# Moving stores to another queue, k casts to another engine and weight loads to a later point in a linear-attention + MLP kernel

## The chip, the cores and the metric

The kernel runs on one core of one Trainium2 chip. The metric is the time of one execution in microseconds (us) on the device. A profiled execution also has a span, which is shorter than its time; positions such as "at 54.27" are microseconds from the start of the span.

The engines are TensorE (PE; its weight loads are PEld), VectorE (DVE), ScalarE (ACT), GpSimd (POOL) and SyncE (SP). Each works through its own list of instructions in order, as the stall described below shows. Tiles whose names begin with `ps_` lie in PSUM, the memory into which TensorE's results go here. A semaphore is a counter on which an instruction waits until another has raised it. A DMA is a transfer between memories; it is issued from one engine's list; a "q" behind an engine's name (ACTq, SPq) marks the engine's sequencer, which does the issuing.

A run counts as slow when it is over 1.5% above the fastest of its kernel; ratios and the medians below are of fast runs.

## The reference, cut to what matters

Causal linear attention with a decay, over 4 batches, 8 heads, 768 positions and a head size of 64, and then an MLP on its 3072 x 512 output.

```python
for b in range(nb):                       # blocks of 64 positions
    intra = einsum('bhic,bhjc->bhij', qb, kb) * Dmask     # decay lam^(i-j), causal
    intra = einsum('bhij,bhjd->bhid', intra, vb)
    inter = einsum('bhid,bhde->bhie', qb * lam_pow, kv_state)
    out[:, :, sl] = intra + inter
    kv_state = lam_block * kv_state + einsum('bhsd,bhse->bhde', kb * rev_pow, vb)
x = out.transpose(0, 2, 1, 3).reshape(3072, 512)
h = x @ w_in                              # 512 x 2048
g = h / (1 + exp(-1.702 * h))
return g @ w_out                          # 2048 x 512, float32
```

## The kernel before

The work is cut into six waves of 128 positions (512 tokens with the four batches). A wave's attention is done in four head pairs. A pair has four steps: casts, transposes (`step_a`), scores, mask and state (`step_b`), and the attention output (`step_c`). Wave 0's attention stands alone at the start, while weights load. The attention of each later wave is interleaved with the MLP of the wave ahead of it, so that TensorE has matmuls to do between the steps.

```python
def do_cast(w, p):
    kf, qf, vf = loaded.pop((w, p))
    ...
    for h in range(2):
        hd = 2 * p + h
        nc.vector.tensor_scalar(ks[:, :, h, :], kf[:, :, h, :], scalar1=k_pow[:, hd : hd + 1], scalar2=None, op0=MUL)
        if w <= 1:
            nc.scalar.activation(qs[:, :, h, :], qf[:, :, h, :], COPY, scale=q_pow[:, hd : hd + 1])
        else:
            nc.vector.tensor_scalar(qs[:, :, h, :], ...)
    nc.gpsimd.tensor_copy(v_sb[w % 2][p][:, :, 0:3:2, :], vf)

def step_a(w, p):                    # 8 transposes of ks and qs, then one copy out of PSUM
    ...
    nc.vector.tensor_copy(kq, ps_t)

def step_b(w, p):                    # 8 score matmuls, 2 masks, 4 state matmuls, 2 state updates
    ...
    nc.vector.scalar_tensor_tensor(sm, s2[h], inv_pow[...], mask.to_broadcast([P, B, P]), op0=MUL, op1=MUL)
    ...
    nc.vector.scalar_tensor_tensor(new[hs, :, hs], old[hs, :, hs], blk_pow[...], ps_kv[hs, :, hs], op0=MUL, op1=ADD)

def mlp2(w, g, j):
    ...
    if j == FFC // CW - 1:
        o = op.tile([P, d_model], f32, tag="o", name="o_sb")
        nc.vector.tensor_copy(o, ps_out)
        (nc.sync if w else nc.scalar).dma_start(out=out[r0 : r0 + P, :], in_=o)     # wave 0: on ScalarE

...
for p in range(NP):                  # wave 0
    do_cast(0, p)
    if p == 2:
        load_weights()               # 3 w_in and 4 w_out chunks, issued by GpSimd
        sync_behind_weights()        # SyncE waits for the third w_out chunk
        load(1)                      # wave 1's k, q, v, issued by SyncE
    step_a(0, p)
    if p:
        step_c(0, p - 1)
    step_b(0, p)
...                                  # then 8 memsets on GpSimd (v_sb and kv_sb of wave 1)
...                                  # wave w's main list: 19 mlp1 items, 16 mlp2 items; load(w + 2) at its start
```

## Time and profile before

The median of the runs is 260.73 us (260.08 to 260.99).

The page of the profile gives each engine's busy time, then the busy share in forty slices of 6.5 us, in tenths. PEclk is the clock that TensorE was granted, in tenths of full speed.

```profile
PE 219.7 (84%) x1478; PEld 115.6 (44%) x1504; DVE 104.8 (40%) x208; ACT 85.1 (33%) x153; POOL 27.2 (10%) x59
...
PE   0374899807665899999999999999999999999993
...
PEclk9999999975777999999999999999999999999999
```

TensorE is at nine tenths or more nearly throughout after the first 14 slices. What can be won lies in the first 14 slices, and there are two weak places: the beginning, and the stretch from about 50 to 90 us.

The same, cut by stage (the windows view): wave 0's attention; wave 0's MLP as far as it runs alone; wave 1's attention; and the first 35 us of the steady waves. The columns are the window, its length, the busy time of each engine with its instructions, the granted clock, the DMA share and GB/s.

```profile
core 0: us, PE busy (x) PEld busy (x) DVE busy (x) ACT busy (x) POOL busy (x), PEclk, DMA share, GB/s
0.00:26.90 26.90, 11.30 (x105) 8.55 (x107) 12.38 (x20) 12.77 (x27) 14.98 (x39) 1.00 0.98 191
26.90:51.00 24.10, 23.07 (x109) 10.61 (x111) 2.56 (x5) 10.49 (x19) 1.22 (x2) 1.00 0.99 190
51.00:88.10 37.10, 20.31 (x145) 10.97 (x146) 15.03 (x29) 5.18 (x11) 5.52 (x9) 0.72 0.90 210
88.10:123.60 35.50, 34.30 (x258) 18.68 (x263) 18.23 (x39) 12.26 (x21) 0.61 (x1) 1.00 0.10 34
```

The steady stretch has TensorE busy for 34.30 of 35.50 us. Wave 1's attention is the outlier: 37.10 us long, TensorE busy for 20.31, at a mean clock of 0.72.

What happens there (the timeline; columns: start, duration, engine, line, operation, out<-in, shape and count, and in brackets the idle time before it and what ended that):

```profile
46.05 0.69 DVE L236 COPY o_sb<-ps_out 128x512 f32<-128x512 f32 x1 [18.50 <-PE ps_out L232]
...
51.03 0.39 PE L167 MATMUL ps_t<-ident,ks 128*128 128x128 bf16 x4
...
54.27 4.48 ACTq L238 DMA_DIRECT2D out_dram<-o_sb  x2
...
58.79 0.91 ACT L156 ACTIVATE qs<-qf,q_pow 128x256 bf16<-128x256 f32 x2 [15.60 <-DMA qf<-in_q_dram]
...
59.76 0.61 PE L167 MATMUL ps_t<-ident,qs 128*128 128x128 bf16 x4 [8.34 <-ACT qs L156]
...
63.71 0.61 PE L180 MATMUL ps_s<-kq 64*128 64x128 bf16 x8
...
66.75 0.62 DVE L154 TENSOR_SCALAR ks<-kf,k_pow 128x256 bf16<-128x256 f32 x2
...
67.43 0.40 PE L167 MATMUL ps_t<-ident,ks 128*128 128x128 bf16 x4 [2.57 <-DVE ks L154]
...
70.62 0.61 PE L180 MATMUL ps_s<-kq 64*128 64x128 bf16 x8
```

There are two troubles.

**A store in front of a cast.** The first output tile of wave 0 is ready at 46.05 + 0.69 = 46.74. Its store issues only at 54.27. ScalarE's next instruction, the q cast of wave 1's first pair, runs at 58.79, after two stores, and TensorE stands for 8.34 us for want of it. Why a store waits is told by the order of instructions in the built program with the semaphores that each waits for (not a profile):

```
SyncE     44 L79 DMACopy qf<-in_q_dram 128x4x64 [waits DMAHW6_49]
SyncE     50 L79 DMACopy qf<-in_q_dram 128x4x64 [waits DMAHW4_49,Activation_49]
ScalarE   31 L238 DMACopy out_dram<-o_sb 128x512 [waits DMAHW6_49,DVE_49]
ScalarE   32 L238 DMACopy out_dram<-o_sb 128x512 [waits DMAHW4_49,DVE_49]
ScalarE   33 L156 Activation qs<-qf,q_pow 128x4x64
```

The program rotates eight semaphores among all DMAs issued by SyncE and ScalarE, and a DMA waits until the one that used its semaphore last has landed. So the first store waits for a load of wave 1's last pair, and the second for a load of wave 2, although it needs neither's data. The chain of waits (start, duration, what) names the second of these loads:

```profile
54.56 3.71 DMA qf<-in_q_dram
...
58.35 0.40 ACTq L238
...
58.79 0.92 ACT qs L156 x2
```

The Trainium skill, "DMA: Bandwidth & Descriptors", section "Anatomy of one DMA — SWDGE (gpsimd) path", says that the DMA engines themselves don't wait on semaphores: any such wait happens on the issuing sequencer before the DMA is dispatched. That is what makes the wait costly here. It stands in ScalarE's list, and the trace agrees: ScalarE's arithmetic is idle for 15.60 us ahead of the q cast at 58.79.

**A ring of one pair after another.** The scores of the first two pairs are at 63.71 and 70.62, 6.91 us apart. The next pair's k cast is in VectorE's list behind this pair's mask (1.40 us) and state update (0.98), so the next transposes come 3.7 us after the scores (67.43), and their copy and the next scores come behind those.

**The beginning.** The timeline of the last pair of wave 0, by engine:

```profile
20.71 2.91 DVE L154 TENSOR_SCALAR ks<-kf,k_pow 128x256 bf16<-128x256 f32 x2
...
20.23 0.36 POOL L298 MEMSET v_sb_145<- 128x256 bf16 x1
...
22.64 0.58 POOL L298 MEMSET kv_152<- 128x512 bf16 x1
...
26.87 1.48 PE L222 MATMUL ps_h<-xT,w_in_157 128*128 128x512 bf16 x5 [0.22 <-issue]
```

Two k casts take 2.91 us here and 0.62 at 66.75. During the long ones GpSimd runs eight memsets.

### The profile page before, as it was taken

To read this page: it belongs to the slowest core of one execution; us is meant where nothing else is said; L and a number is where in the kernel's file an instruction comes from. 1 tells how busy PE (TensorE), PEld (TensorE's weight loads), DVE (VectorE), ACT (ScalarE), POOL (GpSimd) and SP (SyncE) were. 2 spreads that over 40 slices of the span, in tenths; PEclk is the share of its full clock that TensorE was granted. 3 is DMA by queue.
4 is the path that set the end of the run, shared out by engine and by line. 5 is a ranking of instruction groups with operands and counts; after the bars stand their busy time and mean duration, and the time that the engine had idled before them with its cause. 6 is when DMAs were issued, how large, how long until landed. Compare 5 with 4: busy or idle time off the path is not lost.

```text
span 260.2 us, 3823 instructions
## 1 busy us (share of the span) xinstructions
PE 219.7 (84%) x1478; PEld 115.6 (44%) x1504; DVE 104.8 (40%) x208; ACT 85.1 (33%) x153; POOL 27.2 (10%) x59
## 2 busy tenths in 40 slices
PE   0374899807665899999999999999999999999993
PEld 0253444403333445555455554555554455544441
DVE  0457200202455947371854555564527425110121
ACT  6543564001320165311455012551106530146200
POOL 6185000011111000000011000010000000000000
PEclk9999999975777999999999999999999999999999
DMA  5999997999997200012795114990111001210022
GB/s 134 235 192 204 205 160 175 212 247 263 233 240 170 65 20 3 0 40 83 176 221 130 40 43 125 235 205 3 54 69 40 0 3 42 83 40 0 0 83 81
DMA packets 83350, 29.62 MB, mean 114 GB/s; under 512 B 76676, under 2 KB 79748, under 8 KB 83332
## 3 DMA queue, kind: packets, MB, share of 16 engines
q1 hardware_dynamic: 79060, 24.13, 37.6%
q0 software_dynamic: 3696, 4.19, 9.8%
q10 hardware_dynamic: 576, 1.05, 1.1%
q8 instruction: 12, 0.20, 0.3%
q14 instruction: 6, 0.05, 0.1%
HBM read 27.27 MB, written 6.29 MB: 129 GB/s over the span
## 4 chain that ended last, share of the span: by engine, by line
PE 69%; DMA 10%; SPq 9%; DVE 3%; issue 3%; ACT 2%; POOL 1%; ACTq 0%; DVEq 0%; POOLq 0%
PE ps_out L232 30%; PE ps_h L222 26%; SPq L79 9%; DMA w_out_162<-in_moe_w_out_dram 8%; PE ps_t L167 4%; PE ps_o L209 4%; PE ps_s L180 3%; PE ps_kv L189 2%; PE ps_o L207 2%; DMA qf<-in_q_dram 1%; DMA vf<-in_v_dram 1%; ACT g_sb L225 1%; DVE sm L183 1%; DVE ks L154 1%; DVE o_sb L236 1%
## 5 line engine op out<-in xcount | busy, mean ns | idle before, releaser
L225 ACT ACTIVATE g_sb<-ps_h 128x512 bf16<-128x512 f32 x96 | 56.0, 597 | 54.4 <-PE ps_h L222 53.6
L232 PEld LDWEIGHTS <-g_sb 128*128 128x128 bf16 x384 | 37.4, 101 | 40.5 <-issue 3.3
L183 DVE SCALAR_TENSOR_TENSOR sm<-ps_s,inv_pow,mask 128x512 bf16<-128x512 f32 x48 | 33.8, 747 | 34.6 <-PE ps_s L180 34.6
L236 DVE COPY o_sb<-ps_out 128x512 f32<-128x512 f32 x24 | 16.6, 691 | 73.2 <-PE ps_out L232 73.0
L222 PE MATMUL ps_h<-xT,w_in_159 128*128 128x512 bf16 x185 | 44.7, 379 | 0.4
L212 ACT CAST xT<-ps_o 128x512 bf16<-128x512 f32 x24 | 14.0, 585 | 76.0 <-PE ps_o L209 75.6
L169 DVE COPY kq<-ps_t 128x1024 bf16<-128x1024 bf16 x24 | 16.6, 692 | 38.5 <-PE ps_t L167 38.5
L167 PE MATMUL ps_t<-ident,ks 128*128 128x128 bf16 x96 | 10.2, 234 | 20.6 <-DVE ks L154 20.6
L222 PEld LDWEIGHTS <-w_in_159 128*128 128x128 bf16 x192 | 18.1, 98 | 19.1
L232 PE MATMUL ps_out<-w_out_162,g_sb 128*128 128x512 bf16 x95 | 26.0, 398 | 0.2 <-issue 0.2
L222 PE MATMUL ps_h<-xT,w_in_157 128*128 128x512 bf16 x94 | 23.1, 381 | 3.6 <-ACT g_sb L225 1.5
L232 PE MATMUL ps_out<-w_out_160,g_sb 128*128 128x512 bf16 x94 | 24.9, 387 | 0.3 <-issue 0.2
L232 PE MATMUL ps_out<-w_out_161,g_sb 128*128 128x512 bf16 x91 | 24.6, 390 | 0.3
L232 PE MATMUL ps_out<-w_out_163,g_sb 128*128 128x512 bf16 x91 | 24.5, 391 | 0.3
L222 PE MATMUL ps_h<-xT,w_in_158 128*128 128x512 bf16 x92 | 22.8, 379 | 0.2
L154 DVE TENSOR_SCALAR ks<-kf,k_pow 128x256 bf16<-128x256 f32 x48 | 18.5, 400 | 5.5 <-ACT k_pow L105 5.3
L167 PEld LDWEIGHTS <-ks 128*128 128x128 bf16 x96 | 7.3, 103 | 26.1 <-DVE ks L154 22.1
L167 PE MATMUL ps_t<-ident,qs 128*128 128x128 bf16 x96 | 10.5, 238 | 10.0 <-ACT qs L156 10.0
L222 PEld LDWEIGHTS <-w_in_157 128*128 128x128 bf16 x96 | 9.5, 99 | 15.7 <-issue 6.1
L156 ACT ACTIVATE qs<-qf,q_pow 128x256 bf16<-128x256 f32 x16 | 7.2, 500 | 20.9 <-DMA qf<-in_q_dram 20.8
L222 PEld LDWEIGHTS <-w_in_158 128*128 128x128 bf16 x96 | 9.1, 98 | 9.4
L180 PE MATMUL ps_s<-kq 64*128 64x128 bf16 x192 | 11.2, 247 | 0.8 <-DVE kq L169 0.8
(108 smaller groups left out, 151.5 us busy)
## 6 DMA issues: line engine op xcount, KB each, us to landing
kf<-in_k_dram SPq DMA_DIRECT2D x48, 128.0 KB, 3.0
qf<-in_q_dram SPq DMA_DIRECT2D x48, 128.0 KB, 3.0
vf<-in_v_dram SPq DMA_DIRECT2D x48, 128.0 KB, 3.0
out_dram<-o_sb SPq DMA_DIRECT2D x20, 256.0 KB, 2.0
w_in_159<-in_moe_w_in_dram POOLq DMA_DIRECT2D x1, 1024.0 KB, 14.8
out_dram<-o_sb ACTq DMA_DIRECT2D x4, 256.0 KB, 3.3
w_in_157<-in_moe_w_in_dram POOLq DMA_DIRECT2D x1, 512.0 KB, 7.8
w_in_158<-in_moe_w_in_dram POOLq DMA_DIRECT2D x1, 512.0 KB, 9.4
```

The lines of the kernel that those rows point to most:

```text
L79: nc.sync.dma_start(out=x[:, :, h, :], in_=src[:, 2 * p + h, w * P : (w + 1) * P, :].rearrange("b s d -> s b d"))
L154: nc.vector.tensor_scalar(ks[:, :, h, :], kf[:, :, h, :], scalar1=k_pow[:, hd : hd + 1], scalar2=None, op0=MUL)
L167: nc.tensor.transpose(ps_t[:, i, b, :], x[:, b, :], ident)
L169: nc.vector.tensor_copy(kq, ps_t)
L180: nc.tensor.matmul(s2[h][:, b, :], kq[hs, 0, b, :], kq[hs, 1, b, :], start=True, stop=True)
L183: nc.vector.scalar_tensor_tensor(sm, s2[h], inv_pow[:, 2 * p + h : 2 * p + h + 1], mask.to_broadcast([P, B, P]), op0=MUL, op1=MUL)
L209: nc.tensor.matmul(ps_o[:, b, :], vt[:, b, h : h + 2, :].rearrange("p c d -> p (c d)"), masked[w, p, h][:, b, :], start=(not w and h == 0) ...
L212: nc.scalar.copy(x, ps_o.rearrange("p b s -> p (b s)"))
L222: nc.tensor.matmul(h_ps[fc], w_in_sb[j][:, kc, i * P : (i + 1) * P], xT[w, kc], start=(kc == 0), stop=(kc == KC - 1))
L225: nc.scalar.activation(g_of[w][:, fc, :], h_ps.pop(fc), GELU)
L232: nc.tensor.matmul(ps_out, g_of[w][:, fc, g * P : (g + 1) * P], w_out_sb[j][:, fc % CW, :], start=(fc == 0), stop=(fc == FFC - 1))
L236: nc.vector.tensor_copy(o, ps_out)
```

## The change

It has four parts. (1) `w_in` comes in five chunks instead of three; the first is issued behind the arrival of the last pair's q, the others behind that pair's v cast. (2) All stores are issued by SyncE; wave 2's loads are placed behind the first two of them. (3) The k casts of wave 1 go to GpSimd. (4) In wave 0 two output groups are computed side by side, and the attention of later waves is spread a little later over the main list.

```diff
-    IN_COLS = [4, 4, 8]
+    IN_COLS = [2, 2, 4, 4, 4]
...
+    def load_weights_first():
+        nc.gpsimd.tensor_copy(behind_q, loaded[0, NP - 1][1][0:1, 0, 1, 0:1])
+        load_w_in(0)
+
     def load_weights():
...
+        for j in range(1, len(IN_COLS)):
+            load_w_in(j)
         for j, x in enumerate(w_out_sb):
...
-            nc.vector.tensor_scalar(ks[:, :, h, :], kf[:, :, h, :], scalar1=k_pow[:, hd : hd + 1], ...)
+            eng = nc.gpsimd if w == 1 else nc.vector
+            eng.tensor_scalar(ks[:, :, h, :], kf[:, :, h, :], scalar1=k_pow[:, hd : hd + 1], ...)
...
-            (nc.sync if w else nc.scalar).dma_start(out=out[r0 : r0 + P, :], in_=o)
+            nc.sync.dma_start(out=out[r0 : r0 + P, :], in_=o)
...
+    def mlp2_items(w):
+        nj = FFC // CW
+        if w == 0:
+            return ([(mlp2, w, g, j) for j in range(nj) for g in range(2)]
+                    + [(mlp2, w, g, j) for g in range(2, G) for j in range(nj)])
+        return [(mlp2, w, g, j) for g in range(G) for j in range(nj)]
...
         for p in range(NP):
+            if p == NP - 1:
+                load_weights_first()
             do_cast(0, p)
-            if p == 2:
+            if p == NP - 1:
                 load_weights()
                 sync_behind_weights()
                 load(1)
...
-                    side += [(n + 8 + 2 * i, s) for i, s in enumerate(attn_steps(w + 1))]
+                    side += [(n + 12 + 1.9 * i, s) for i, s in enumerate(attn_steps(w + 1))]
             if w + 2 < NW:
-                side += [(n, (load, w + 2))]
+                side += [(n if w else EARLY + FFC + 2 * (FFC // CW), (load, w + 2))]
```

More of the change, by code (lines that the diff above doesn't have):

```diff
@@ L127, with load_w_in @@
     in_of = [(j, i) for j, c in enumerate(IN_COLS) for i in range(c)]
-    def load_weights():
-        f0 = 0
-        for j, x in enumerate(w_in_sb):
-            f1 = f0 + IN_COLS[j] * P
-            nc.gpsimd.dma_start(out=x, in_=moe_w_in.rearrange("(kc ki) f -> ki kc f", ki=P)[:, :, f0:f1])
-            f0 = f1
+    def load_w_in(j):
+        f0 = sum(IN_COLS[:j]) * P
+        nc.gpsimd.dma_start(
+            out=w_in_sb[j], in_=moe_w_in.rearrange("(kc ki) f -> ki kc f", ki=P)[:, :, f0 : f0 + IN_COLS[j] * P])
+    def load_weights_first():
+        nc.gpsimd.tensor_copy(behind_q, loaded[0, NP - 1][1][0:1, 0, 1, 0:1])
+        load_w_in(0)
+    def load_weights():
+        for j in range(1, len(IN_COLS)):
+            load_w_in(j)
         for j, x in enumerate(w_out_sb):
@@ L139 @@
     behind = const.tile([1, 2], bf16)
+    behind_q = const.tile([1, 1], f32)
     def sync_behind_weights():
@@ L153, in do_cast @@
             hd = 2 * p + h
-            nc.vector.tensor_scalar(ks[:, :, h, :], kf[:, :, h, :], scalar1=k_pow[:, hd : hd + 1], scalar2=None, op0=MUL)
+            eng = nc.gpsimd if w == 1 else nc.vector
+            eng.tensor_scalar(ks[:, :, h, :], kf[:, :, h, :], scalar1=k_pow[:, hd : hd + 1], scalar2=None, op0=MUL)
             if w <= 1:
@@ L246, in mlp_items @@
                 + [(mlp1, w, fc, first + last) for fc in range(EARLY, FFC)]
-                + [(mlp2, w, g, j) for g in range(G) for j in range(FFC // CW)])
+                + mlp2_items(w))
     def attn_steps(w):
```

## The prediction

> **What bounds the kernel now.** TensorE is busy 84% of 260.2 us (page, part 1), but from 100 to 220 us it is busy 39.4 to 39.5 of every 40 us (windows): from 88 us on the waves are matmul-bound, about 35 us each, The loss lies before.
>
> - Wave 1's attention (timeline, 51 to 88 us). TensorE stands still from 51.4 to 59.76, because the transpose of q waits for ScalarE's q cast, and that stands behind two output stores in ScalarE's queue. The first store's tile was ready at 46.7, yet it issues at 54.27, the second near 58.7. The instruction order shows each store waiting on a DMA semaphore shared with a load eight DMAs earlier on SyncE's queue; the chain of waits shows the second (load 54.56, 3.71 us, then the cast at 58.79).
> - Then each of the four pairs takes 6.9 us (score matmuls at 63.71, 70.62, 77.48, 84.38), because VectorE runs a ring: mask 1.41, state 0.98, next k cast 0.62, transpose, copy 0.69. TensorE is half-clocked in part: granted 0.51 from 60 to 65, 0.77 from 65 to 80 (windows). The Trainium skill, "TensorE: Matmul & The Clock Gate", Part 1, explains half rate by idleness; this trace agrees (a 512-column matmul starts every 0.43 us there, 0.215 later).
> - Prologue. The last pair's k cast takes 2.91 us instead of 0.61 while GpSimd runs eight memsets (20.23 to 23.2). The Trainium skill, "SBUF — State Buffer", "Who interferes with whom", says such a VectorE cast and a GpSimd instruction exclude each other.
>
> **What the change does.**
> 1. Weight issues behind the last pair's q move the memsets from 20.2 to about 24, after that cast: prologue 2.2 us shorter, first MLP matmul at 24 instead of 26.3. The weight stream was saturated anyway (2.57 us per 512 KB chunk): the first chunk lands near 20, the third w_out chunk near 39, as now, so wave 1's loads start at 39 and its last v lands near 56, unchanged.
> 2. Stores on SyncE free ScalarE: the 8.3 us stall goes.
> 3. The k casts leave VectorE's ring: mask 1.41 + state 0.98 + copy 0.69 + score latency gives about 3.5 us a pair instead of 6.9. GpSimd's cast is estimated at 0.4 to 0.7 us (its v cast, twice as wide, takes 0.61), below the 3.6 us between pairs' arrivals.
> 4. Wave 2's loads start after two stores, near 53.5 as now, land near 70; its steps begin 12 items in, near 76.
>
> Walking TensorE's order with these durations: MLP of wave 0 from 24.1, first transpose of wave 1 at 48.7, scores at 51.1, 55.3, 58.9, 62.4; MLP of wave 1 from 63.7, its third accumulation (which waits for the last output copy) at 65.8 instead of 88.1. Nearly all 22.3 us are critical, since the rest is matmul-bound. 1 us is kept for cold matmuls: 239 us.
>
> **What shows it.** First MLP matmul near 24; no store on ScalarE; TensorE gap near 50 gone; pairs 3.3 to 4 us apart; granted clock near 1 from 48 on; later waves still about 35 us.
>
> **What would make it wrong.** GpSimd's scaled cast taking over 1.5 us; wave 1's loads starting later than 41, so that arrivals pace the pairs; TensorE staying half-clocked in wave 1 (up to +6 us); load 2 landing late and holding VectorE; later attention steps stalling at wave ends.
>
> Faster by over 2%: 0.96; within 2%: 0.03; slower: 0.01. Range 234 to 246.

## The result, and the profile after

The changed kernel takes 239.32 us (median of 4, 238.85 to 240.31); the kernel before, run beside it, 260.86 us (260.08 to 261.18). The ratio is 0.918, with a 95% interval from 0.915 to 0.922. Ratios here are the mean time of one kernel's fast runs over that of the other's of the same rounds, so not quite the ratio of the medians. The profile before is of an execution of 261.98 us and the profile after of one of 238.85, so the two profiles differ by 23 us where the medians differ by 21.5. All outputs are right.

The page of the changed kernel, the same three rows (a slice is now 5.9 us):

```profile
PE 214.9 (91%) x1504; PEld 113.0 (48%) x1504; DVE 100.4 (42%) x200; ACT 85.3 (36%) x153; POOL 36.2 (15%) x70
...
PE   0367899989889999999999999999999999999993
...
PEclk9999999999999999999999999999999999999999
```

The hole in the PE row is gone, and so is the dip in the granted clock. The same four stages (windows, columns as before; a DMA share above 1 is as the tool prints it, and nothing here rests on it):

```profile
0.00:24.00 24.00, 11.04 (x104) 8.33 (x105) 9.45 (x19) 12.60 (x26) 13.28 (x34) 1.00 0.97 164
24.00:48.40 24.40, 23.47 (x116) 10.73 (x114) 2.52 (x4) 11.67 (x21) 6.75 (x13) 1.00 1.12 199
48.40:65.00 16.60, 14.24 (x147) 8.44 (x146) 13.16 (x23) 4.38 (x9) 6.96 (x9) 1.00 1.13 235
65.00:100.50 35.50, 34.56 (x263) 18.67 (x263) 18.67 (x39) 12.26 (x21) 4.29 (x7) 1.00 0.80 170
```

The stages went from 26.90 to 24.00, from 24.10 to 24.40, from 37.10 to 16.60, and stayed at 35.50. In these two profiles, then, 20.5 us come from wave 1's attention and 2.9 from the beginning. (TensorE's own busy time in wave 1's attention fell by 6 us for the same work, from 20.31 to 14.24: those matmuls now run at full clock.)

The timeline of wave 1's attention:

```profile
43.39 1.83 POOL L163 TENSOR_SCALAR ks<-kf,k_pow 128x256 bf16<-128x256 f32 x2 [15.97 <-DMA kf<-in_k_dram]
...
44.44 1.03 ACT L165 ACTIVATE qs<-qf,q_pow 128x256 bf16<-128x256 f32 x2 [3.89 <-DMA qf<-in_q_dram]
...
48.62 0.39 PE L176 MATMUL ps_t<-ident,qs 128*128 128x128 bf16 x4
...
50.66 0.40 PE L189 MATMUL ps_s<-kq 64*128 64x128 bf16 x8
...
51.23 0.39 PE L176 MATMUL ps_t<-ident,ks 128*128 128x128 bf16 x4
...
54.45 0.40 PE L189 MATMUL ps_s<-kq 64*128 64x128 bf16 x8
```

The q cast runs at 44.44, four microseconds before TensorE wants it. The transposes of the second pair come 0.57 us after the first pair's scores (51.23), where they came 3.72 us after before. The beginning:

```profile
20.60 0.60 DVE L163 TENSOR_SCALAR ks<-kf,k_pow 128x256 bf16<-128x256 f32 x2
...
24.43 0.37 POOL L317 MEMSET v_sb_145<- 128x256 bf16 x1
...
24.03 1.69 PE L231 MATMUL ps_h<-xT,w_in_157 128*128 128x512 bf16 x6
```

The memsets start at 24.43, behind the weight issues (about 0.75 us of GpSimd each), and the k casts take 0.60 us.

### The profile page after: what moved, and what is told of

The parts are those of the page before. It is cut to its first block, busy times and chain, and to the rows that moved or that the text cites. A ratio compares the mean times of both kernels' runs of the same rounds, so it can differ in the third digit from the quotient of the medians.

```text
span 237.2 us, 3855 instructions
## 1 busy us (share of the span) xinstructions
PE 214.9 (91%) x1504; PEld 113.0 (48%) x1504; DVE 100.4 (42%) x200; ACT 85.3 (36%) x153; POOL 36.2 (15%) x70
## 4 chain that ended last, share of the span: by engine, by line
PE 87%; DVE 5%; ACT 4%; issue 2%; DMA 1%; DVEq 0%; ACTq 0%
PE ps_out L241 35%; PE ps_h L231 34%; PE ps_o L218 5%; PE ps_t L176 5%; PE ps_s L189 4%; DVE sm L192 3%; PE ps_kv L198 2%; PE ps_o L216 2%; ACT g_sb L234 2%; DMA lam_p<-in_lam_dram 1%; DVE ks L163 1%; DVE o_sb L245 1%; ACT L280 1%; ACT L105 1%; ACT xT L221 1%
## 5 line engine op out<-in xcount | busy, mean ns | idle before, releaser
L241 PEld LDWEIGHTS <-g_sb 128*128 128x128 bf16 x384 | 35.9, 98 | 36.9
L241 PE MATMUL ps_out<-w_out_165,g_sb 128*128 128x512 bf16 x96 | 24.5, 379 | 0.0
L241 PE MATMUL ps_out<-w_out_163,g_sb 128*128 128x512 bf16 x96 | 24.5, 379 | 0.0
L241 PE MATMUL ps_out<-w_out_162,g_sb 128*128 128x512 bf16 x96 | 24.5, 379 | 0.0
L241 PE MATMUL ps_out<-w_out_164,g_sb 128*128 128x512 bf16 x96 | 24.5, 379 | 0.0
L231 PE MATMUL ps_h<-xT,w_in_161 128*128 128x512 bf16 x96 | 23.0, 379 | 0.0
L231 PE MATMUL ps_h<-xT,w_in_160 128*128 128x512 bf16 x96 | 23.0, 379 | 0.0
L231 PE MATMUL ps_h<-xT,w_in_159 128*128 128x512 bf16 x96 | 21.7, 379 | 0.0
L176 PE MATMUL ps_t<-ident,ks 128*128 128x128 bf16 x96 | 10.2, 234 | 10.6 <-DVE ks L163 10.6
L163 DVE TENSOR_SCALAR ks<-kf,k_pow 128x256 bf16<-128x256 f32 x40 | 13.6, 349 | 7.1 <-ACT k_pow L105 5.3
L231 PE MATMUL ps_h<-xT,w_in_158 128*128 128x512 bf16 x48 | 13.3, 378 | 2.2 <-ACT g_sb L234 1.5
L231 PEld LDWEIGHTS <-w_in_159 128*128 128x128 bf16 x96 | 9.4, 98 | 11.3
L231 PE MATMUL ps_h<-xT,w_in_157 128*128 128x512 bf16 x48 | 12.5, 384 | 1.3 <-ACT xT L221 1.3
L231 PEld LDWEIGHTS <-w_in_160 128*128 128x128 bf16 x96 | 9.1, 98 | 9.4
L231 PEld LDWEIGHTS <-w_in_161 128*128 128x128 bf16 x96 | 9.0, 98 | 9.6
L167 DVE TENSOR_SCALAR qs<-qf,q_pow 128x256 bf16<-128x256 f32 x32 | 11.1, 348 | 1.5 <-DMA qf<-in_q_dram 1.5
```

What stands on the lines that cost most here:

```text
L163: eng.tensor_scalar(ks[:, :, h, :], kf[:, :, h, :], scalar1=k_pow[:, hd : hd + 1], scalar2=None, op0=MUL)
L167: nc.vector.tensor_scalar(qs[:, :, h, :], qf[:, :, h, :], scalar1=q_pow[:, hd : hd + 1], scalar2=None, op0=MUL)
L176: nc.tensor.transpose(ps_t[:, i, b, :], x[:, b, :], ident)
L231: nc.tensor.matmul(h_ps[fc], w_in_sb[j][:, kc, i * P : (i + 1) * P], xT[w, kc], start=(kc == 0), stop=(kc == KC - 1))
L241: nc.tensor.matmul(ps_out, g_of[w][:, fc, g * P : (g + 1) * P], w_out_sb[j][:, fc % CW, :], start=(fc == 0), stop=(fc == FFC - 1))
```

## The experiments

The theory: the stall at the q cast, the ring of pairs and the memset collision are three separate losses, removed by parts 2, 3 and 1; part 4 is worth little. Rivals: that the stores' traffic costs, not the wait in ScalarE's list; that the k casts matter only because TensorE had gone cold behind the stall; that the beginning gives its 2.7 us whatever follows.

Two positions tell the first two losses apart in every trace: when the first scores of wave 1 come, and how long it is from the first to the fourth. The last columns are the first MLP matmul of wave 1 (it decides, since what follows is alike), and the timed runs with ratios to the kernel before.

| kernel | first scores | first to fourth | wave 1's MLP | median us (range) | ratio, 95% interval |
|---|---|---|---|---|---|
| before | 63.71 | 20.67 | 86.22 | 260.86 to 261.87 (medians of five series) | 1 |
| b_stores | 53.25 | 21.60 | 76.28 | 252.23 (251.81 to 252.56) | 0.963, 0.960 to 0.967 |
| b_storepool | 53.56 | 20.63 | 76.11 | 251.83 (251.46 to 252.95) | 0.963, 0.959 to 0.966 |
| b_kcast | 62.73 | 11.08 | 75.24 | 251.24 (251.05 to 251.31) | 0.959, 0.957 to 0.962 |
| b_memset | 62.42 | 20.96 | 84.80 | 261.95 (261.27 to 262.85) | 1.001, 0.997 to 1.005 |
| changed | 50.66 | 10.83 | 62.92 | 239.32 (238.85 to 240.31) | 0.918, 0.915 to 0.922 |
| after_again | 51.51 | 10.84 | 63.77 | 239.75 (239.01 to 239.93) | 0.915, 0.912 to 0.919 |
| a_store_act | 55.10 | 13.48 | 70.01 | 244.77 (243.58 to 246.09) | 0.935, 0.930 to 0.940 |
| a_kcast_dve | 50.95 | 21.39 | 73.82 | 249.67 (249.36 to 251.29) | 0.955, 0.949 to 0.961 |
| a_w_early | 51.34 | 10.83 | 63.60 | 240.29 (239.53 to 240.92) | 0.918, 0.913 to 0.923 |
| a_w_before | 54.34 | 10.83 | 66.60 | 241.37 (239.29 to 242.52) | 0.921, 0.915 to 0.927 |
| a_rest | 51.44 | 10.83 | 63.70 | 240.74 (239.97 to 241.33) | 0.920, 0.915 to 0.924 |
| i_pipe | 51.17 | 10.83 | 63.43 | 238.16 (237.59 to 239.37) | 0.910, 0.906 to 0.913 |
| i_best | 47.04 | 10.84 | 59.30 | 235.15 (234.18 to 235.88) | 0.899, 0.896 to 0.902 |

Names with b_ are the kernel before with one part of the change; names with a_ are the changed kernel with one part undone.

### b_stores: the stores alone

```diff
-            (nc.sync if w else nc.scalar).dma_start(out=out[r0 : r0 + P, :], in_=o)
+            nc.sync.dma_start(out=out[r0 : r0 + P, :], in_=o)
```

> The kernel before with one edit: wave 0's four output stores go out on SyncE's queue, behind wave 2's loads, instead of ScalarE's. Theory (ScalarE is held by the store's semaphore wait): the 8.3 us gap of TensorE near 51 to 60 us is gone and the pairs of wave 1 still pace at 5.6 to 6.9 us because the k casts stay in VectorE's ring; 248 to 253 us. Rival (the second half of the loss is a consequence of the gap, by the half clock alone): pairs at about 4 us, 242 us or less.

```profile
43.04 0.89 ACT L156 ACTIVATE qs<-qf,q_pow 128x256 bf16<-128x256 f32 x2
...
53.25 0.40 PE L180 MATMUL ps_s<-kq 64*128 64x128 bf16 x8
```

The first pair's q cast runs at 43.04 instead of 58.79. The first scores came 10.5 us earlier and the time fell by 9.6 us (261.87 to 252.23, medians of the same series). The pairs did not come closer: 21.60 us from the first to the fourth, or 7.05 to 7.40 us each, a little more than the 5.6 to 6.9 expected. This part removes the stall and leaves the ring.

### b_storepool: the stores on GpSimd instead

```diff
-            (nc.sync if w else nc.scalar).dma_start(out=out[r0 : r0 + P, :], in_=o)
+            (nc.sync if w else nc.gpsimd).dma_start(out=out[r0 : r0 + P, :], in_=o)
```

> The kernel before with wave 0's four stores on GpSimd's queue: the store traffic stays at 47 to 55 us, beside wave 1's loads, but no engine that casts q waits and no semaphore is shared with the loads. Theory (a queue held by a wait): as fast as with the stores on SyncE, within 2 us. Rival (the q cast is late because store traffic slows the q load): as slow as the kernel before, 260 us.

The stores now go out even earlier than in the kernel before, while wave 1's loads are still arriving (timeline):

```profile
47.30 0.57 POOL L238 DMA_DIRECT2D out_dram<-o_sb  x1 [23.80 <-DVE o_sb L236]
...
51.52 0.39 PE L167 MATMUL ps_t<-ident,qs 128*128 128x128 bf16 x4
```

The first store issues at 47.30 rather than 54.27, and q's transposes run at 51.52 rather than 59.76. The time is that of b_stores within the intervals. So the traffic of the stores at that moment costs nothing that shows, and neither does it matter which other queue carries them. What cost was the wait ahead of the q cast in ScalarE's list.

### b_kcast: the k casts alone

```diff
-            nc.vector.tensor_scalar(ks[:, :, h, :], ...)
+            eng = nc.gpsimd if w == 1 else nc.vector
+            eng.tensor_scalar(ks[:, :, h, :], ...)
```

> The kernel before with one edit: wave 1's k casts on GpSimd. Theory (two losses in series): the gap until 59.8 us stays, then pairs at about 3.5 to 4 us instead of 6.9; saves about 9 us, 250 to 253 us. Rival (ScalarE's later stores pace the pairs too): pairs stay above 5 us, 256 us or more.

The stall stays and the ring goes:

```profile
53.53 4.24 ACTq L239 DMA_DIRECT2D out_dram<-o_sb  x2
...
58.78 0.61 PE L168 MATMUL ps_t<-ident,qs 128*128 128x128 bf16 x4 [6.12 <-ACT qs L157]
```

TensorE still waits for q, for 6.12 us, but from the first scores to the fourth it is then 11.08 us instead of 20.67, and the time falls by 10.6 us. That is against the rival which holds that the ring was slow only because TensorE had gone cold: here TensorE comes out of the same stall just as cold (the four transposes at 58.78 take 0.61 us, not 0.39), and the pairs are still fast.

### b_memset: the memsets alone, out of the way

```diff
             do_cast(0, p)
+            if p == 0:
+                for i in range(NP):
+                    nc.gpsimd.memset(v_sb[1][i][:, :, 1, :], 0.0)
+                    nc.gpsimd.memset(kv_sb[0][i], 0.0)
...
-        for i in range(NP):
-            side += [(4, (nc.gpsimd.memset, v_sb[1][i][:, :, 1, :], 0.0)), (4, (nc.gpsimd.memset, kv_sb[0][i], 0.0))]
```

> The kernel before with GpSimd's eight memsets for wave 1's buffers moved ahead to 7.5 to 10.5 us, where VectorE runs no SBUF to SBUF cast. Theory (port lock, and prologue time is eaten by the later gap): the last k cast of the prologue takes 0.61 instead of 2.91 us, the first MLP matmul comes at about 24.5 instead of 26.9 us, but the time stays within 1 us of 260.7, because TensorE then waits for the same q cast at 59.8. Rival for the lock: the cast stays near 2.9 us. Rival for the rest: the whole 2.3 us shows in the time.

The local effect is complete, and there is no gain in time (timeline):

```profile
20.72 0.61 DVE L154 TENSOR_SCALAR ks<-kf,k_pow 128x256 bf16<-128x256 f32 x2
...
24.14 2.40 PE L222 MATMUL ps_h<-xT,w_in 128*128 128x512 bf16 x9
...
58.55 0.61 PE L167 MATMUL ps_t<-ident,qs 128*128 128x128 bf16 x4 [9.58 <-ACT qs L156]
```

The casts take 0.61 us again, and the first MLP matmul comes at 24.14 instead of 26.87. But TensorE then waits 9.58 us for the q cast where it waited 8.34. The stall ends with the landing of a load, not a fixed time after the beginning, so starting earlier mostly makes the wait longer. In this one trace wave 1's MLP is still 1.4 us ahead; the timed runs show no difference (ratio 1.001, interval 0.997 to 1.005, which is about 1 us each way). The trace also settles the cause of the long cast: only the memsets were moved, and it became short.

### a_store_act: the stores back on ScalarE

```diff
-            nc.sync.dma_start(out=out[r0 : r0 + P, :], in_=o)
+            (nc.sync if w else nc.scalar).dma_start(out=out[r0 : r0 + P, :], in_=o)
```

> The changed kernel with wave 0's four stores back on ScalarE's queue. Theory: the q casts of wave 1 are held again, TensorE stands about 5 to 8 us near 50 us; 244 to 248 us. Rival (the stores mattered only with the k casts on VectorE): within 1 us of 239.3.

```profile
53.04 0.40 PE L176 MATMUL ps_t<-ident,qs 128*128 128x128 bf16 x4 [2.89 <-ACT qs L165]
...
58.11 0.61 PE L176 MATMUL ps_t<-ident,qs 128*128 128x128 bf16 x4 [2.06 <-ACT qs L165]
```

The time rises by about 5 us, half of what the same edit gives from the other side. The stall is back but shorter: q's transposes wait 2.89 us at 53.04 and 2.06 us at 58.11. The changed kernel places wave 2's loads behind the first two stores, so those stores share their semaphores with loads of wave 1, which land earlier. (The chain of waits shows one such case: a v load of wave 1 takes from 51.48 to 56.69, and the third store issues at 56.76.) How much a store holds its queue depends on which DMA used its semaphore last.

### a_kcast_dve: the k casts back on VectorE

```diff
-            eng = nc.gpsimd if w == 1 else nc.vector
+            eng = nc.vector
```

> The changed kernel with wave 1's k casts back on VectorE. Theory (ring): pairs of wave 1 at 5.6 us with TensorE at full clock, 6.9 at half clock, instead of 3.5; three to four pairs make 6 to 13 us, 246 to 252 us. Rival: the stall was all the stores' doing, within 2 us of 239.3.

```profile
54.66 0.40 PE L176 MATMUL ps_t<-ident,ks 128*128 128x128 bf16 x4 [2.99 <-DVE ks L163]
```

The first scores are where they were (50.95), from the first scores to the fourth it is 21.39 us again, and TensorE waits 2.99 us for VectorE's k cast. The time rises by about 10 us. So the ring needs no stall ahead of it to be slow; it cools TensorE by itself (granted clock 0.79 from 50 to 66 us, where the changed kernel has 1.00). How much of a pair's 7 us is the order of the steps, and how much the half clock that comes with it, no run separates.

### a_w_early and a_w_before: the weight issues back in their old place

```diff
-            if p == NP - 1:
-                load_weights_first()
             do_cast(0, p)
-            if p == NP - 1:
+            if p == 2:
+                load_w_in(0)
                 load_weights()
```

> The changed kernel with all weight issues back in front of the third pair's v cast, as before (still in five chunks), so that the memsets run at about 20 us again. Theory: the last k cast takes 2.9 us again, the first MLP matmul comes at 26.3 to 26.9 us instead of 24.0, and here it costs the time, since nothing after it waits for a fixed event: plus 2 to 3 us, 241 to 242.5 us. Rival (wave 1 is paced by the arrival of its loads): within 0.7 us of 239.3.

This first attempt tested less than it was meant to. I had kept the five chunks of `w_in`. Two more issues on GpSimd pushed the memsets back to 22.35, after the k casts had ended (20.25 + 1.24), so the collision was not brought back and the time did not move: inconclusive for the collision. (Why these casts took 1.24 us and not 0.60, with no memset beside them, stays open.) It does show that wave 1's loads, released 1.6 us earlier here, are not what wave 1 waits for: its first scores came at 51.34. The second restores the three chunks as well:

```diff
-    IN_COLS = [2, 2, 4, 4, 4]
+    IN_COLS = [4, 4, 8]
```

> The changed kernel with the weights wholly as before: w_in in three chunks, all seven issues in front of the third pair's v cast. In the run with early issues but five chunks the memsets came at 22.35 us and missed most of the last k cast (1.24 us), so the collision was not restored; with seven issues they come at 20.2 us. Theory: the last k cast takes 2.9 us, the first MLP matmul comes at 26.3 to 26.9 us, and the time is 1.5 to 2.7 us above the changed kernel's of this call. Rival (wave 1 is paced by the arrival of its loads, which come 1.6 us earlier here): within 0.7 us of it.

```profile
20.20 3.97 DVE L163 TENSOR_SCALAR ks<-kf,k_pow 128x256 bf16<-128x256 f32 x2
...
26.99 2.18 PE L231 MATMUL ps_h<-xT,w_in 128*128 128x512 bf16 x5
```

The long cast is back (3.97 us), the first MLP matmul is at 26.99, and the mean of the fast runs is 1.6 us above that of after_again in the same series (241.1 and 239.6). The size is uncertain: the four fast runs spread from 239.29 to 242.52, two more were slow, though no die or clock marks them as such (with them the difference of the means is 2.2 us), and the intervals of the ratios overlap a little (0.915 to 0.927 and 0.912 to 0.919). The traces are plainer: wave 1's MLP is 2.8 us apart (66.60 and 63.77), as much as the first MLP matmul (26.99 and 24.05), and so are the two profiled executions (242.52 and 239.71). So the delay of the beginning, which a wait for a load mostly swallows in the kernel before, passes through to wave 1 here. By the timed runs it is worth some 1.5 us, with zero not clearly excluded.

### a_rest: the order of groups, loads and later steps undone

```diff
-        if w == 0:
+        if False:
             return ([(mlp2, w, g, j) for j in range(nj) for g in range(2)]
...
-                    side += [(n + 12 + 1.9 * i, s) ...]
+                    side += [(n + 8 + 2 * i, s) ...]
-                side += [(n if w else EARLY + FFC + 2 * (FFC // CW), (load, w + 2))]
+                side += [(n, (load, w + 2))]
```

> The changed kernel with its three order edits undone together: wave 0's output groups one after the other, wave 2's loads ahead of the stores, attention of later waves 8 items in. Theory: these are worth at most 2 us, 239 to 241.5 us. Rival (the one order on the queue is where the gain is): 245 us or more.

The ratio is 0.920 against the changed kernel's 0.918 and 0.915 in its own two series: some 0.5 and 1.2 us, with overlapping intervals, so no difference is established. The trace shows small waits of TensorE ahead of the later attention steps, such as 0.66 us for a `kq` copy at 73.72, which the trace of the changed kernel doesn't have there.

### after_again: the changed kernel, unedited

> The changed kernel as it is, once more, so that the other runs of this call have it beside them on the same chip: a ratio of 0.915 to 0.921 to the kernel before.

239.75 us, as in the first series. In this run the scores came about 0.85 us later than in the first profile (51.51). The difference arises in the first nine MLP matmuls: at 24.05, nine take 3.16 us. In the traces of b_memset and a_store_act the same nine take 2.40 and 3.71 us. Such a difference is about the size of the spread between runs.

### i_pipe and i_best: a further step

i_pipe puts each pair's casts of wave 0 ahead of the masking step of the pair before it (the diff shows the lines added, not those removed), so that the next k cast doesn't stand behind this pair's mask on VectorE.

```diff
+        do_cast(0, 0)
         for p in range(NP):
+            step_a(0, p)
+            if p:
+                step_c(0, p - 1)
+            if p + 1 == NP - 1:
+                load_weights_first()
+            if p + 1 < NP:
+                do_cast(0, p + 1)
+            if p + 1 == NP - 1:
+                load_weights(); sync_behind_weights(); load(1)
             step_b(0, p)
```

> The changed kernel with one move: in wave 0 the casts of pair p+1 stand in front of the masking of pair p instead of behind it, so that the transposes of p+1 overlap the masking. Theory: what remains is a chain in the prologue of 4.5 us a pair; with the casts ahead the last scores come at 20 to 22 us instead of 23.1, the MLP starts at 21 to 23 us (its second chunk of w_in lands at 23.8), and all later events move with it: 1 to 3 us off, 236.5 to 238.5 us. Rival (arrivals of wave 1's loads or of the weights now pace it): within 0.7 us of the changed kernel.

238.16 us, 1.6 us below after_again of the same series, though the two ranges overlap (the profile is of the slowest of the six runs, 239.37 us, and shows only 0.34 us of it). The attention of wave 0 ends earlier, but the MLP then waits for its weights: 1.50 us for the first chunk (its matmuls run at 20.84) and 1.19 us for the next (24.77). It also runs at a lower clock there, granted 0.69 from 20.8 to 30 us. i_best therefore issues three chunks ahead of the last v cast, without waiting for q. It also puts the last output copy of wave 0 on ScalarE, for the 0.63 us that the third accumulation of wave 1 waited for it on VectorE.

```diff
-        nc.gpsimd.tensor_copy(behind_q, ...)
-        load_w_in(0)
+        for j in range(3):
+            load_w_in(j)
...
-            nc.vector.tensor_copy(o, ps_out)
+            (nc.scalar.copy if w == 0 and g == G - 1 else nc.vector.tensor_copy)(o, ps_out)
```

> The run with the casts ahead, with two more edits: the first three chunks of w_in are issued in front of the last pair's v cast without waiting for its q, and the last output copy of wave 0 is made by ScalarE. In the run with the casts ahead the MLP began at 20.84 us but stood 1.50 and 1.19 us for the first two chunks, and TensorE waits 0.63 us for the last output copy behind VectorE's state update. Theory (arrival of the weights is the limit now): no wait for w_in above 0.5 us, and 1.5 to 3 us off the run with the casts ahead: 235 to 237 us, a ratio of 0.898 to 0.905. Rival (the early weights only delay the last q, k and v by as much): 237.6 us or more.

```profile
20.82 1.92 PE L230 MATMUL ps_h<-xT,w_in 128*128 128x512 bf16 x8 [1.77 <-DMA w_in<-in_moe_w_in_dram]
...
59.30 2.11 PE L230 MATMUL ps_h<-xT,w_in 128*128 128x512 bf16 x9
```

235.15 us, ratio 0.899: it beats both kernels. Not all went as expected. The first chunk was still waited for, 1.77 us, so the MLP starts no earlier than in i_pipe. What was won is the wait for the second chunk, an earlier release of wave 1's loads (its first v cast is at 44.37, in i_pipe at 46.84), and the wait for the output copy (nine matmuls in a row at 59.30). TensorE also runs at full clock from 20.8 to 30 us (granted 1.00, in i_pipe 0.69) and does 43 matmuls in that stretch instead of 26. How the 3 us divide among these was not taken apart.

## Why the prediction was right

- **The bound.** It said that everything from 88 us on is bound by matmuls, about 35 us a wave, so what is won earlier stays won. The steady stretch is 35.50 us long in both kernels.
- **The stall.** It put the 8.3 us down to the stores in ScalarE's list. b_stores removed the stall alone (first scores 10.5 us earlier, 9.6 us of time); b_storepool showed that the wait, not the traffic, is the cause.
- **The ring.** It added mask, state, copy and score latency to about 3.5 us a pair; the second to fourth pairs of the changed kernel are 3.52 us apart (54.45, 57.97, 61.49). b_kcast and a_kcast_dve tie this to the k casts from both sides (10.6 and about 10 us).
- **The beginning.** Predicted: memsets near 24, first MLP matmul near 24. Measured: 24.43 and 24.03. (Its "26.3" for the kernel before is where the weight load for that matmul starts; the matmul itself is at 26.87, so the beginning became shorter by 2.8 us and not by 2.2.)
- **The walk through TensorE's order.** Scores predicted at 51.1, 55.3, 58.9 and 62.4; measured at 50.66, 54.45, 57.97 and 61.49. Third accumulation predicted at 65.8, measured at 65.01. The kept 1 us for cold matmuls was used up by ordinary runs: the first profile is of the fastest of the four runs (238.85), and after_again's scores (51.51 to 62.35) are the predicted ones almost exactly.

Smaller terms were off. GpSimd's k cast was estimated at 0.4 to 0.7 us, from its v cast; it takes 0.92 us (the group of instructions, with minimum, median and maximum in ns):

```profile
L163 DVE TENSOR_SCALAR ks<-kf,k_pow x40: 344/348/356, 5.3 to 175.3; 128x256 bf16<-128x256 f32 x40
L163 POOL TENSOR_SCALAR ks<-kf,k_pow x8: 912/922/925, 43.4 to 55.9; 128x256 bf16<-128x256 f32 x8
```

The error did no harm: two k casts and a v cast take 1.83 + 0.61 = 2.44 us of GpSimd for a pair, and the v casts, which wait for v to arrive, are 3.4 to 4.3 us apart (46.68, 50.99, 54.44, 57.81). Wave 2's loads started at 55.80, not 53.5; VectorE waited up to 1.31 us for some of them (70.81), TensorE for none. Wave 1's loads started at 40.60, not 39, close to the 41 that the prediction named as a danger, and the last pair's v cast ran at 57.81, not near 56. That these arrivals don't set the pace is seen in i_best: there the loads start at 37.95, and from the first scores to the fourth it is 10.84 us all the same.

What the prediction did not say is how the parts depend on each other. It counted the beginning as worth its full length. It can count only together with the stores: alone it was worth nothing measurable (b_memset), because the stall swallowed it. The parts alone give 9.6, 10.6 and 0 us, together 20.2, against the 21.5 us that the change gives (260.86 to 239.32). The remaining 1.3 us is of the size that a_w_before measured for the beginning once the stall is gone, within the uncertainty of both. But part 4, which is in neither sum, may hold some of it (0.5 to 1.2 us by a_rest, not clear of zero), so the 1.3 us are not shown to be the beginning.

## What to carry to other kernels

Don't put a DMA that may have to wait in the list of an engine whose next instruction is urgent; and look up which DMA it shares a semaphore with, as the data it carries may have nothing to do with its wait. A gain ahead of a wait for an arrival is not visible until that wait is gone, so judge each part of a change with and without the others, as here with the memsets (nothing alone, some 1.5 us in company). When a pair of steps repeats slowly, list what stands between one step and the next on the in-order engine: moving a cast that itself takes 0.62 us to an engine on which it takes 1.83 us made each pair 3.4 us shorter.

## What the Trainium skill lacked or had wrong

- No page has the wait of one queue's store for another queue's load through a shared, rotating DMA semaphore. Here eight of them serve two queues, and the store of a tile that was ready at 46.74 issued at 54.27. ("DMA: Bandwidth & Descriptors" would be the place.)
- "GPSIMD Engine Reference", section 4.1, "Engine selection", calls GpSimd "roughly line-rate" for operations of one input. Here a scaled cast of 128x256 from f32 to bf16 took 0.92 us on GpSimd and 0.35 on VectorE, while an unscaled cast of twice the width took 0.61 on GpSimd. So it depends on the operation: the scaled one costs about three times as much per element as the plain one. (The profile's spans on GpSimd are rough, but two scaled casts in a row take 1.83 us.)
- "SBUF — State Buffer", section "Who interferes with whom", says that a VectorE cast in a mode with two ports and a GpSimd instruction exclude each other for a whole instruction. The trace agrees that they exclude each other (b_memset). But the cast was held through a whole run of memsets of 0.35 to 0.58 us each, not through one: two casts took 2.91 us in the kernel before, one of them alone 2.66, and 3.97 in a_w_before, against 0.60. That successive memsets leave no gap for the cast is an inference, and so is that this cast is in such a mode; no run took either apart.
- "TensorE: Matmul & The Clock Gate", Part 1, puts half speed down to idleness, and the traces agree (granted 0.51 from 60 to 65 us behind the stall, 1.00 in each of the four stages of the changed kernel). Its warning that the clock's trace events can't be wholly trusted is borne out as well: PEclk says 1.00 up to 26.9 us, yet in that stretch eight score matmuls take 0.61 us, as behind the stall, and 0.40 in the changed kernel's wave 1.
